# Where the causal mask of two score blocks is written, and in which order the transposed probabilities are copied

## The chip, the cores and the metric

The kernel runs on one core of a Trainium2 chip. A core has engines with instruction queues of their own: TensorE (PE in the profile; its weight loads are listed as PEld), VectorE (DVE), ScalarE (ACT), GpSimd (POOL) and SyncE (SP), which here issues nearly all DMAs. Each engine takes its instructions strictly in the order in which they were written and waits on semaphores of the others. The metric is the device time of one execution in microseconds. The kernel before took 1091.67 us, the median of three runs (1091.38 to 1092.66).

## The reference

Attention with a decay, and behind it a gated feed-forward layer on all 4608 tokens. The sizes: batch 8, 8 heads, 576 positions, head dimension 64; model dimension 512, hidden dimension 2048; all in float32.

```python
def _attn_ref(q, k, v, f):
    scores = scale * np.matmul(q, k.transpose(0, 1, 3, 2))
    log_f = np.log(np.clip(f, 0.0001, 1.0))
    cum = np.cumsum(log_f, axis=-1)
    decay = cum[:, :, :, None] - cum[:, :, None, :]
    causal = np.triu(np.ones((S, S), dtype=bool), k=1)
    scores = np.where(causal, -1000000000.0, scores + decay)
    scores = scores - np.max(scores, axis=-1, keepdims=True)
    attn = np.exp(scores)
    attn = attn / (np.sum(attn, axis=-1, keepdims=True) + 1e-09)
    return np.matmul(attn, v).astype(np.float32)

def _moe_ref(x, w_in, w_out):
    h = x @ w_in
    sp = np.maximum(h, 0.0) + np.log1p(np.exp(-np.abs(h)))
    g = h * erf(sp)
    return (g @ w_out).astype(np.float32)
```

The row's own `cum` cancels in the softmax, so the kernel adds only a term that depends on the key's position. It calls these terms the decays.

## The kernel before

**Two phases.** The first 350 us compute the attention of 64 heads; the rest is the feed-forward layer (class `Moe`), whose lines the change leaves alone. During the attention, the weights of the later phase are also unpacked, combined and written back to memory in small pieces (`convert`), and the first activations are split into high and low parts; that work goes to DVE, ACT and POOL between the attention's own.

**Pairs, halves, steps.** Two heads make a pair p (32 pairs). The 576 rows of a head are cut into five blocks 0 to 4 that end at 64, 192, 320, 448 and 576; because of the causal mask a block i needs only the keys up to its own end. A pair takes two steps t of the loop at L660: the even one has blocks 4 and 1, the odd one blocks 3, 2 and 0. The letter j is the head in the pair.

**A step's pipeline.** In step t the program writes, in this order: `normalize(t - 2)`, `store(t - 5)`, `scores(t)`, the first half of `exps(t - 1)`, the first half of `reduce(t)`, `transposes(t - 3)`, one `evacuate`, `values(t - 4)`, the other halves of `exps` and `reduce`, the other `evacuate`s, and then pieces of the weights' conversion. Since every engine keeps the written order, this order decides who stands behind whom.

- `scores` (L517) is TensorE's: for each block the products of q and k into PSUM (L526), and then for each block and head one constant product (L531): an identity (`eye`) times `upper`, a 128x128 triangle of -2^33 in bfloat16, added onto the block's diagonal. That is the causal mask. There are two PSUM tiles for scores, one per head, so the scores of a step wait for the reductions of the step before.
- `reduce` (L543) is DVE's: it adds the decays `c` to the scores, takes the minimum of the negated row and writes the sum to `pr` in SBUF (L549). Each instruction is followed by a short one that reads the accumulator.
- `exps` (L557) is ACT's, in place in `pr` (L561), with the row's sum.
- `normalize` (L564): DVE adds a small number and takes the reciprocal (L566, L568), POOL multiplies each row block of both heads (L572), in the order of the blocks.
- `transposes` (L575): TensorE turns 128x128 pieces of `pr` into PSUM banks (L584). An even half fills three banks of four pieces, an odd half three banks and a fourth with one piece, that of block 0. There are three bank buffers (`ps_t`).
- `evacuate` (L586) copies a bank to `pt` in SBUF: full banks go to ACT (L593), the third bank of odd halves to DVE (L591), the small fourth bank to DVE (L589, 64 columns).
- `values` (L597) is TensorE's product of `pt` and v (L611), `store` copies it out of PSUM on DVE (L620 to L624) and writes it to memory.

**Decays.** A pair's `c` holds 2 x 576 values, the same in every row, which two DMAs spread over the rows (`load_decays`, L486). They are issued in the even step four steps ahead of the pair's first. Pair 0 has none of them: its decays are made at the start by `spread` (L501) with TensorE and ACT.

**The start.** `lead(n)` (L495) is n products of the identity with itself, whose result nobody reads; each is two instructions in the profile. There are eight at the beginning and four in each of steps 1 and 2.

Of the kernel before, what the change touches and what calls it, by code (L numbers as in the profile page):

```python
# [312 lines left out]
def attention_moe(ctx, tc, q2, k2, vp, f, w_in, w_out, out):  # L313
# [145 lines left out]
    with ExitStack() as ph:  # L459
# [57 lines left out]
        def scores(t):  # L517


            p, half = divmod(t, 2)  # L520
            q, k = pairs[p][:2]
            s = [ps_s.tile([P, 1024], F32, name=f"s{t}_{j}", tag="s") for j in range(2)]
            for at, i, k0, k1 in PARTS[half]:
                for j in range(2):
                    h = slice(64 * j, 64 * j + 64)
                    nc.tensor.matmul(out=s[j][:, at:at + k1 - k0], lhsT=q[h, PAD + START[i]:PAD + END[i]],  # L526
                                     rhs=k[h, k0:k1], start=i > 0, stop=k1 < END[i])
            for j in range(2):
                for i in BLOCKS[half]:
                    first = max(0, START[i])  # L530
                    nc.tensor.matmul(out=s[j][:, SCOL[i] + first:SCOL[i] + END[i]], lhsT=eye,  # L531
                                     rhs=upper[:, first - START[i]:], start=False, stop=i != 3)
            raw_scores[t] = s
            probs[t] = wk.tile([P, TCOLS[half]], F32, name=f"pr{t}", tag=f"pr{half}")
            n = len(BLOCKS[half])
            line = wk.tile([P, 32], F32, name=f"st{t}", tag=f"st{half}")
            stats[t] = line[:, :6 * n].rearrange("p (a j m) -> p a j m", a=3, j=2)

# [36 lines left out]
        def transposes(t, a):  # L575

            half = t % 2
            if a == 0:
                pts[t] = wk.tile([P, 1600 if half else 1536], F32, name=f"pt{t}", tag=f"pt{half}", bufs=1)
# [6 lines left out]
        def evacuate(t, a):  # L586
            b, pt = banks.pop((t, a)), pts[t]
            if a == 3:
                nc.vector.tensor_copy(out=pt[:, 1536:], in_=b[:, 64:128])  # L589
# [4 lines left out]
            if a == len(BANKS[t % 2]) - 1:  # L594
# [56 lines left out]
        lead(8)  # L651
# [8 lines left out]
        for t in range(NH + 2):  # L660
# [11 lines left out]
            if t in (NH - 24, NH - 16):  # L672
                moe.load_wi((t - NH + 24) // 8)
            if there[2]:
                normalize(t - 2)
            if there[5] and t < NH + 2:
# [7 lines left out]
            elif t < 3:  # L684
                lead(4)
# [4 lines left out]
            if there[3]:  # L690
                for a in range(3):
                    transposes(t - 3, a)
                evacuate(t - 3, 0)
            if there[3] and len(BANKS[(t - 3) % 2]) == 4:
                transposes(t - 3, 3)
# [6 lines left out]
            if there[3]:  # L702
                for a in range(1, len(BANKS[(t - 3) % 2])):
# [92 lines left out]
```

## Time and profile before

| what | value |
|---|---|
| time, median of three runs | 1091.67 us (1091.38 to 1092.66) |
| the profiled execution's own time | 1089.61 us |
| its span | 1087.8 us |
| mean granted clock of TensorE | 0.997 |
| loop of the attention, first scores to last | 5.5 to 322 us |
| constant mask products (L531) | 320, in 64 steps |
| granted clock from 12.0 to 18.8 us | 0.50 |
| mean DMA rate over the span | 270 GB/s |

The span is that of one profiled execution. Busy times add up what an engine ran; pipelined matmuls overlap, so starts of rows tell more of TensorE's pace than their lengths. In a row of the timeline, a number in brackets is the idle time in front of it and what ended that.

### The profile page before, as it was taken

How to read it: one execution, taken by the hardware profiler on the slowest of the kernel's cores; microseconds unless marked ns; L12 is line 12 of the kernel's file. 1: busy time of each engine (PE TensorE's matmuls, PEld its weight loads, DVE VectorE, ACT ScalarE, POOL GpSimd, SP SyncE). 2: the span in 40 equal slices, each digit the busy share in tenths (PEclk: the TensorE clock that was granted, in tenths of full speed). 3: DMA queues.
4: the chain of work that ended last, by engine and by line, in shares of the span. 5: the costliest groups of instructions: out<-in, count | busy, mean ns of one | idle time of the engine just before them, and what ended most of it. 6: DMA issues, size and time to landing. Idle time of an engine off the chain costs nothing.

```text
span 1087.8 us, 22066 instructions
## 1 busy us (share of the span) xinstructions
PE 1078.9 (99%) x7592; PEld 952.5 (88%) x7592; DVE 832.0 (76%) x1906; ACT 740.8 (68%) x1593; POOL 703.8 (65%) x824
## 2 busy tenths in 40 slices
PE   8999999999999999999999999999999999999998
PEld 6888888888889889988999888889988998899887
DVE  6788898888765997988897987676776768676665
ACT  4888889888886766567666666666575656656563
POOL 2657678787764969888787878636454554546322
PEclk8999999999999999999999999999999999999999
DMA  8689988899875687887969777785867769584742
GB/s 285 224 260 324 316 294 277 283 352 329 279 227 208 234 304 294 300 331 252 348 240 351 288 265 282 266 307 185 308 248 254 287 229 327 207 321 181 246 190 97
DMA packets 86191, 293.70 MB, mean 270 GB/s; under 512 B 8896, under 2 KB 25280, under 8 KB 73792
## 3 DMA queue, kind: packets, MB, share of 16 engines
q1 hardware_dynamic: 85936, 292.00, 75.7%
q8 instruction: 61, 1.00, 0.3%
q14 instruction: 50, 0.41, 0.1%
q10 hardware_dynamic: 144, 0.29, 0.1%
HBM read 240.73 MB, written 51.53 MB: 269 GB/s over the span
## 4 chain that ended last, share of the span: by engine, by line
PE 94%; DVE 3%; issue 1%; ACT 1%; DMA 1%; SPq 0%; DVEq 0%; ACTq 0%
PE y L234 34%; PE s L526 10%; PE pha L176 9%; PE o L611 9%; PE phx L176 9%; PE phy L176 9%; PE t L584 8%; PE phb L176 4%; PE s L531 2%; DMA xt_d<-xo 1%; DVE u L182 0%; DVE ys L255 0%; DVE pr L549 0%; DVE e L215 0%; DMA k<-in_k_dram 0%
## 5 line engine op out<-in xcount | busy, mean ns | idle before, releaser
L223 POOL TENSOR_TENSOR gl<-e,gh 128x384 fp32r<-128x384 f32 x192 | 217.6, 1165 | 263.3 <-PE y L234 157.4
L234 PE MATMUL y<-wo,gh 128*128 128x512 f32 x1152 | 356.4, 390 | 0.4 <-DVE ys L255 0.3
L234 PEld LDWEIGHTS y<-wo,gh 128*128 128x128 f32 x1152 | 215.0, 188 | 45.5 <-DVE ys L255 1.7
L572 POOL TENSOR_SCALAR pr<-pr,st 128x576 f32<-128x576 f32 (+4 forms) x320 | 164.9, 536 | 104.2 <-DVE st L568 42.7
L234 PE MATMUL y<-wo,gl 128*128 128x512 f32 x576 | 225.1, 391 | 0.0
L255 DVE TENSOR_TENSOR ys<-y,ys 128x512 f32<-128x512 f32 x252 | 172.0, 687 | 55.0 <-PE y L234 53.6
L561 ACT ACTIVATE pr<-pr,st 128x576 f32<-128x576 f32 (+3 forms) x320 | 177.0, 559 | 4.2 <-DVE st L549 4.2
L549 DVE CUSTOM_DVE_ANT_0 pr<-s,c 128x576 f32<-128x576 f32 (+3 forms) x320 | 136.6, 487 | 51.0 <-PE s L531 26.5
L222 ACT CAST gh<-e 128x384 fp32r<-128x384 f32 x192 | 94.0, 513 | 67.2 <-DVE e L215 64.9
L205 ACT ACTIVATE e<-u 128x384 f32<-128x384 f32 x144 | 75.0, 522 | 78.6 <-DVE u L182 75.2
L234 PEld LDWEIGHTS y<-wo,gl 128*128 128x128 f32 x576 | 108.1, 188 | 22.7
L593 ACT COPY pt<-t 128x512 f32<-128x512 f32 x158 | 88.3, 581 | 50.8 <-PE t L584 50.6
L176 PE MATMUL pha<-xs,wi 128*128 128x384 f32 x576 | 116.9, 337 | 0.1
L176 PE MATMUL phx<-xs,wi 128*128 128x384 f32 x576 | 115.4, 334 | 0.0
L176 PE MATMUL phy<-xs,wi 128*128 128x384 f32 x576 | 115.3, 334 | 0.0
L526 PE MATMUL s<-k,q 64*128 64x320 f32 (+4 forms) x768 | 112.6, 412 | 1.6 <-DVE st L549 1.1
L205 ACT ACTIVATE e<-pha 128x384 f32<-128x384 f32 x48 | 23.6, 492 | 125.5 <-PE pha L176 125.5
L176 PEld LDWEIGHTS pha<-xs,wi 128*128 128x128 f32 x576 | 102.3, 188 | 4.2 <-DVE u L186 0.4
L584 PE MATMUL t<-ident,pr 128*128 128x128 f32 x800 | 103.8, 275 | 0.7 <-ACT pt L593 0.6
L611 PE MATMUL o<-pt,v 128*64 128x128 f32 (+1 forms) x1920 | 102.5, 259 | 0.9 <-DVE xo L620 0.9
L611 PEld LDWEIGHTS o<-pt,v 128*64 128x64 f32 x1920 | 93.7, 137 | 10.3 <-DVE st L549 4.4
L526 PEld LDWEIGHTS s<-k,q 64*128 64x128 f32 x768 | 75.1, 189 | 30.3 <-issue 15.2
(73 smaller groups left out, 1758.8 us busy)
## 6 DMA issues: line engine op xcount, KB each, us to landing
wi<-wi_d SPq DMA_DIRECT2D x48, 1792.0 KB, 7.5
wo<-wo_d SPq DMA_DIRECT2D x48, 1024.0 KB, 6.5
v<-in_vp_dram SPq DMA_DIRECT2D x32, 576.0 KB, 4.8
r<-xt_d SPq DMA_DIRECT2D x48, 384.0 KB, 9.1
c<-cum_d SPq DMA_DIRECT2D x62, 288.0 KB, 6.8
q<-in_q_dram SPq DMA_DIRECT2D x32, 320.0 KB, 5.5
k<-in_k_dram SPq DMA_DIRECT2D x32, 288.0 KB, 5.9
part_d<-ys SPq DMA_DIRECT2D x36, 256.0 KB, 6.3
```

What stands on the lines that cost most here:

```text
L176: nc.tensor.matmul(out=ps, lhsT=wi[:, w, n, kd], rhs=xs[:, x, kd], start=not part and kd == 0 and i == 0, stop=kd == 1 and i == 2, skip_gr ...
L205: nc.scalar.activation(out=e_, in_=h[c], func=AF.Softplus)
L222: nc.scalar.copy(out=gh, in_=e_)
L223: nc.gpsimd.tensor_tensor(out=gl, in0=e_, in1=gh.bitcast(F32), op=ALU.subtract)
L234: nc.tensor.matmul(out=y, lhsT=x[:, cs], rhs=wo[:, i, w], start=i == 0 and n == 0, stop=i == 1 and n == 2)
L255: nc.vector.tensor_tensor(out=ys, in0=y, in1=ys, op=ALU.add)
L526: nc.tensor.matmul(out=s[j][:, at:at + k1 - k0], lhsT=q[h, PAD + START[i]:PAD + END[i]], rhs=k[h, k0:k1], start=i > 0, stop=k1 < END[i])
L549: nc.vector.tensor_tensor_reduce(out=to[:, ::-1] if j else to, in0=score, in1=decay_, scale=-0.125, scalar=BIG, op0=ALU.add, op1=ALU.min, ...
L561: nc.scalar.activation(out=seg, in_=seg, func=AF.Exp, bias=st[:, 0, j, m:m + 1], scale=-1.0, accum_out=st[:, 1, j, m:m + 1])
L572: nc.gpsimd.tensor_scalar(out=seg, in0=seg, scalar1=st[:, 2, j, m:m + 1], scalar2=1.0, op0=ALU.mult, op1=ALU.mult)
L584: nc.tensor.transpose(out=b[:, n * P:(n + 1) * P], in_=probs[t][:, at:at + P], identity=ident)
L611: nc.tensor.matmul(out=o[h, to:to + width], lhsT=v[:, ch, h], rhs=pt[:, at[j]:at[j] + width], start=n == 0, stop=n == len(parts) - 1, skip ...
```

## The change

The mask of block 3 in all pairs, and of block 4 in all pairs but the first, no longer goes onto the scores by a product. GpSimd writes the fill value into the decays instead: `mask(p, i)` fills the 128 columns of `c` on the diagonal of block i, for both heads, above the diagonal, with -2^33. It is called in odd steps: block 3 of the same pair ahead of `normalize`, and block 4 of the next pair behind it. The columns of block 3 are also read by block 4's rows (in the even step, without a fill), so their fill comes after those.

In odd halves the small bank with the one piece of block 0 is transposed first and copied first, by ScalarE; the other three banks follow. Only in the last half it stays as it was.

At the start there are eleven constant products instead of eight ahead of the first scores, and four in each of steps 0, 1 and 2.

```diff
@@ scores(t)
                     nc.tensor.matmul(out=s[j][:, at:at + k1 - k0], lhsT=q[h, PAD + START[i]:PAD + END[i]],
-                                     rhs=k[h, k0:k1], start=i > 0, stop=k1 < END[i])
+                                     rhs=k[h, k0:k1], start=i > 0, stop=k1 < END[i] or i == 4 and p > 0)
             for j in range(2):
                 for i in BLOCKS[half]:
+                    if i == 3 or i == 4 and p:
+                        continue
                     first = max(0, START[i])
                     nc.tensor.matmul(out=s[j][:, SCOL[i] + first:SCOL[i] + END[i]], lhsT=eye,
-                                     rhs=upper[:, first - START[i]:], start=False, stop=i != 3)
+                                     rhs=upper[:, first - START[i]:], start=False, stop=True)
...
+        def mask(p, i):
+
+            c = pairs[p][2][:, :, START[i]:END[i]]
+            nc.gpsimd.affine_select(out=c, in_=c, pattern=[[0, 2], [-1, P]], compare_op=ALU.is_ge, fill=MASK,
+                                    base=0, channel_multiplier=1)
@@ transposes(t, a), evacuate(t, a)
-            if a == 0:
+            if t not in pts:
...
             if a == 3:
-                nc.vector.tensor_copy(out=pt[:, 1536:], in_=b[:, 64:128])
+                (nc.vector.tensor_copy if t == NH - 1 else nc.scalar.copy)(out=pt[:, 1536:], in_=b[:, 64:128])
...
-            if a == len(BANKS[t % 2]) - 1:
+            if a == (3 if t == NH - 1 else 2):
                 del probs[t]
@@ before the loop
-        lead(8)
+        lead(11)
@@ the loop
+            if half and there[0]:
+                mask(p, 3)
             if there[2]:
                 normalize(t - 2)
+            if half and t + 1 < NH:
+                mask(p + 1, 4)
...
             if t == 0:
                 spread(pairs[0][2], cum)
-            elif t < 3:
+            if t < 3:
                 lead(4)
...
             if there[3]:
-                for a in range(3):
+                order = range(3) if half else (3, 0, 1, 2)
+                for a in order:
                     transposes(t - 3, a)
-                evacuate(t - 3, 0)
-            if there[3] and len(BANKS[(t - 3) % 2]) == 4:
-                transposes(t - 3, 3)
+                for a in order[:-2]:
+                    evacuate(t - 3, a)
...
             if there[3]:
-                for a in range(1, len(BANKS[(t - 3) % 2])):
+                for a in range(1, 3):
                     evacuate(t - 3, a)
```

Line numbers move in the changed file: L531 is L533 there, L549 is L557, L572 is L580, L584 is L592, and the fill is L544.

On TensorE, an even step (the third pair's) stood like this before: four mask products, the three full banks, then the small one (`t_3`), then the values (`o`).

```order
L531 LDWEIGHTS eye
L531 MATMUL s_0_401<-upper,eye 128x128
L531 LDWEIGHTS eye
L531 MATMUL s_0_401<-upper,eye 128x128
L531 LDWEIGHTS eye
L531 MATMUL s_1_402<-upper,eye 128x128
L531 LDWEIGHTS eye
L531 MATMUL s_1_402<-upper,eye 128x128
L584 MATMUL t_0_421<-ident,pr_255 128x128 x4
L584 MATMUL t_1_426<-ident,pr_255 128x128 x4
L584 MATMUL t_2_431<-ident,pr_255 128x128 x4
L584 MATMUL t_3_437<-ident,pr_255 128x128
```

The same step now:

```order
L533 LDWEIGHTS eye
L533 MATMUL s_0_415<-upper,eye 128x128
L533 LDWEIGHTS eye
L533 MATMUL s_1_416<-upper,eye 128x128
L592 MATMUL t_3_433<-ident,pr_267 128x128
L592 MATMUL t_0_435<-ident,pr_267 128x128 x4
L592 MATMUL t_1_440<-ident,pr_267 128x128 x4
L592 MATMUL t_2_445<-ident,pr_267 128x128 x4
```

Block 4's product of each head is gone (block 1 keeps its own), and the small bank's transpose moved from the end to the front.

On POOL, an odd step had only the six products of `normalize` and then conversion work; `pr` are the probabilities, `st` the row sums, and the names in brackets the engines whose semaphores are waited for.

```order
L572 TENSOR_SCALAR pr_957<-pr_957,st_958 128x448 [waits DVE_49,PE_49,Activation_49]
L572 TENSOR_SCALAR pr_957<-pr_957,st_958 128x448 [waits Activation_49]
L572 TENSOR_SCALAR pr_957<-pr_957,st_958 128x320
L572 TENSOR_SCALAR pr_957<-pr_957,st_958 128x320 [waits Activation_49]
L572 TENSOR_SCALAR pr_957<-pr_957,st_958 128x64
L572 TENSOR_SCALAR pr_957<-pr_957,st_958 128x64 [waits Activation_49]
```

The same step now, with the fill of block 3 in the pair's `c` ahead, and that of block 4 in the next pair's `c` behind:

```order
L544 AFFINE_SELECT c_715<-c_715 128x2x128 [waits DVE_49]
L580 TENSOR_SCALAR pr_979<-pr_979,st_980 128x448 [waits DVE_49,PE_49,Activation_49]
L580 TENSOR_SCALAR pr_979<-pr_979,st_980 128x448 [waits Activation_49]
L580 TENSOR_SCALAR pr_979<-pr_979,st_980 128x320
L580 TENSOR_SCALAR pr_979<-pr_979,st_980 128x320 [waits Activation_49]
L580 TENSOR_SCALAR pr_979<-pr_979,st_980 128x64
L580 TENSOR_SCALAR pr_979<-pr_979,st_980 128x64 [waits Activation_49]
L544 AFFINE_SELECT c_878<-c_878 128x2x128 [waits DMAHW5_49,DMAHW4_49]
```

The first fill waits for DVE, the second for the two DMAs that bring the decays; everything that follows on POOL stands behind both.

At the start, TensorE's order behind the first step's scores was:

```order
L507 MATMUL spread_223<-cum,first 128x512
L507 MATMUL ends<-cum,first 128x64
L507 MATMUL spread_228<-cum,first 128x512
L507 MATMUL ends<-cum,first 128x64
L526 MATMUL s_0_241<-k_168,q_167 128x448
L526 MATMUL s_1_242<-k_168,q_167 128x448
```

Now it is:

```order
L507 MATMUL spread_226<-cum,first 128x512
L507 MATMUL ends<-cum,first 128x64
L507 MATMUL spread_231<-cum,first 128x512
L507 MATMUL ends<-cum,first 128x64
L499 MATMUL lead<-ident 128x128 x4
L526 MATMUL s_0_255<-k_168,q_167 128x448
```

Four constant products stand between the spread and the scores of step 1.

## The prediction

> **What bounds the kernel.** I read the page first: the engines' shares, then the chain that ended last. (In the rows PE is TensorE, PEld its weight loads, DVE VectorE, ACT ScalarE, POOL GpSimd.)
>
> ```profile
> PE 1078.9 (99%) x7592; PEld 952.5 (88%) x7592; DVE 832.0 (76%) x1906; ACT 740.8 (68%) x1593; POOL 703.8 (65%) x824
> ...
> PE 94%; DVE 3%; issue 1%; ACT 1%; DMA 1%; SPq 0%; DVEq 0%; ACTq 0%
> ```
>
> TensorE is busy 99% of the span and is 94% of the chain. Work taken off it shortens the run, as long as nobody makes it wait instead. The change touches only the attention, so I read the chain there in order of time; a row is start, length, line and count.
>
> ```profile
> 31.16 1.66 PE s L526 x12
> ...
> 129.62 1.66 PE s L526 x12
> ...
> 251.58 1.66 PE s L526 x12
> ...
> 286.10 1.50 PE s L526 x12
> ...
> 290.97 1.66 PE s L526 x12
> ...
> 295.95 1.50 PE s L526 x12
> ...
> 320.51 1.66 PE s L526 x12
> ```
>
> The 1.50 rows open even steps, the 1.66 rows odd ones. Undisturbed, an even step lasts 290.97 - 286.10 = 4.87 us and an odd one 4.98 us: 9.85 us a pair. From 31.16 to 320.51 stand 29 pairs, 285.7 us at that pace, and they took 289.35: 3.7 us were lost. All of it lies between 129.62 and 251.58, where 12 pairs took 121.96 us instead of 118.2. Busy time by stretch (columns: length, PE, PEld, DVE, ACT, POOL, clock, DMA share, GB/s):
>
> ```profile
> 31.00:129.00 98.00, 98.00 (x1185) 82.14 (x1183) 79.33 (x317) 83.42 (x254) 62.26 (x111) 1.00 0.85 274
> 129.00:247.00 118.00, 116.64 (x1389) 98.40 (x1387) 102.85 (x375) 102.51 (x303) 97.17 (x155) 1.00 0.89 305
> ```
>
> Ahead of the middle stretch TensorE has no gap at all and POOL is at 64%. In the middle one DVE and ACT are at 87%, POOL at 82%, and they sometimes come late. So TensorE's work is what counts, with less reserve in the middle. What follows the attention, two thirds of the span, holds none of the edited lines, and I leave it as it is.
>
> **The constant products.** A block 3 loses its mask product in all 32 pairs, block 4 in 31, for two heads each: 64 + 62 = 126 products go.
>
> ```profile
> 207.18 0.40 PE L531 MATMUL s<-upper,eye 128*128 128x128 bf16 x4
> 207.41 1.73 PE L584 MATMUL t<-ident,pr 128*128 128x128 f32 x13
> 209.07 0.44 PE L611 MATMUL o<-pt,v 128*64 128x128 f32 x4
> ...
> 212.21 0.46 PE L531 MATMUL s<-upper,eye 128*128 128x128 bf16 x6
> 212.50 1.51 PE L584 MATMUL t<-ident,pr 128*128 128x128 f32 x12
> 213.94 0.44 PE L611 MATMUL o<-pt,v 128*64 128x128 f32 x4
> ```
>
> Lengths overlap in the pipeline, so I use starts. Four products hold TensorE from 207.18 to 207.41, 0.23 us, or 0.0575 each; six, two of them half as wide, take 0.29, the same rate. 126 x 0.0575 = **-7.2 us**. Masks of the other blocks stay, so the change of operand type before them stays too.
>
> **The small bank.** In an even step thirteen transposes take 209.07 - 207.41 = 1.66 us; in an odd one twelve take 1.44, or 0.12 each. The thirteenth thus costs 0.22: 0.10 is a wait. There are three buffers, and the fourth bank waits for the first to be copied out:
>
> ```profile
> 208.11 0.59 ACT L593 COPY pt<-t 128x512 f32<-128x512 f32 x1 [0.45 <-PE t L584]
> L509 ACT COPY c<-ends 128x64 f32<-128x64 f32 x2 | 0.4, 220 | 0.0
> ```
>
> The copy of a full bank runs until 208.70 and only then can the thirteenth go. With the small bank first, its one transpose is done about 0.4 us earlier than four are, its copy takes 0.22 us, inside the 0.45 us for which ACT stood idle, and the bank is needed only after nine transposes, 1.1 us in. So I let the wait go in all 31 such steps: **-3.1 us**; the ends are 0 and, with the longer waits of the middle stretch, 3.8. DVE loses such a copy in 31 steps, ACT gains 31 x 0.22 us. A price stands against it: the small bank needs the last two normalized rows, so its transpose now waits for the end of POOL's six products instead of the first.
>
> **The fill on POOL.** 63 fills come in, two a pair.
>
> ```profile
> L328 POOL TENSOR_SCALAR_AFFINE_SELECT low<-low 128x128 f32<-128x128 f32 x1 | 0.3, 292 | 0.1
> L572 POOL TENSOR_SCALAR pr<-pr,st 128x192 f32<-128x192 f32 x64 | 26.4, 425 | 0.0
> L572 POOL TENSOR_SCALAR pr<-pr,st 128x64 f32<-128x64 f32 x64 | 20.6, 338 | 0.0
> c<-cum_d SPq DMA_DIRECT2D x62, 288.0 KB, 6.8
> ```
>
> The same operation on half the elements takes 0.29 us. 128 more elements cost another POOL operation 0.09 us, which gives 0.38; twice the work gives 0.58. I take 0.4. The decays land 6.8 us after their issue and are issued about three steps, 14 us, before the fill of block 4: no wait there. The fill of block 3 waits for the reductions of the step before, which read those columns; the reductions of its own step wait for it.
>
> ```profile
> 309.28 0.35 DVE L549 CUSTOM_DVE_ANT_0 pr<-s,c 128x192 f32<-128x192 f32 x1
> 310.89 2.84 POOL L572 TENSOR_SCALAR pr<-pr,st 128x448 f32<-128x448 f32 x6 [2.81 <-ACT pt L593]
> 312.71 0.63 DVE L549 CUSTOM_DVE_ANT_0 pr<-s,c 128x448 f32<-128x448 f32 x1 [1.58 <-PE s L531]
> ...
> 202.65 3.29 POOL L572 TENSOR_SCALAR pr<-pr,st 128x448 f32<-128x448 f32 x6
> 205.90 1.16 POOL L412 TENSOR_TENSOR wa<-wa 128x256 f32<-128x256 f32 x1
> ```
>
> In the quiet part the old step's reductions end at 309.63 and the new ones start at 312.71; POOL idles for 2.81 us in between. The fill hides whole, 2.6 us ahead of its reader, and at 313.73 the second fill goes behind the six products and ahead of the weights' subtractions, which nobody on the path awaits. In the middle stretch POOL can have no gap, as from 202.65 on: there the first fill ends near 203.05, the six products at 206.34 instead of 205.94, still 1.1 us before the transposes at 207.41. What is lost there is what queues up. POOL's work grows to 97.2 + 24 x 0.4 = 106.8 us in 118.0 - 12 x 0.33 = 114.0 us (a pair gains 0.23 in products and 0.10 in the wait), 94%; ACT's to 102.5 + 12 x 0.22 = 105.1, 92%. The stretch lost 3.8 us at 82 and 87%; I take 40% more, **+1.5 us**, from ends of 0 and 4.0, its whole gain.
>
> **The start.** Three constant products more ahead of the first scores, four more behind the spread, and the clock:
>
> ```profile
> 1.36 3.78 PE L499 MATMUL lead<-ident 128*128 128x128 f32 x16 [1.36 <-POOL ident masks.py:199]
> 5.54 1.57 PE L526 MATMUL s<-k,q 64*128 64x320 f32 x12 [0.40 <-DMA k<-in_k_dram]
> 9.40 0.33 PE L507 MATMUL ends<-cum,first 64*128 64x64 f32 x2
> 10.44 3.80 PE L526 MATMUL s<-k,q 64*128 64x448 f32 x12 [0.71 <-DVE st L549]
> 16.69 2.81 PE L526 MATMUL s<-k,q 64*128 64x320 f32 x12
> 19.67 1.11 PE L499 MATMUL lead<-ident 128*128 128x128 f32 x8
> 20.95 2.65 PE L526 MATMUL s<-k,q 64*128 64x448 f32 x12 [0.17 <-DVE st L549]
> 5.20:12.00 6.80, 5.66 (x30) 3.36 (x32) 4.00 (x12) 3.10 (x9) 0.00 (x0) 1.00 0.68 241
> 12.00:18.80 6.80, 6.80 (x33) 5.85 (x31) 4.44 (x18) 4.16 (x17) 0.05 (x1) 0.50 0.84 272
> ```
>
> One such product is two instructions: 0.22 us each at the beginning, 0.12 later. Six more from 5.14 end between 5.9 and 6.4, where the scores began at 5.54, and the spread stands right behind those: **+0.4** of 0 to 0.9. The other eight take 1.0 us, from about 9.5; scores waited until 10.44 anyway: **+0.1**. From 12.0 to 18.8 the granted clock is 0.50, after a stretch in which TensorE was busy 5.66 of 6.80 us. The step that ran in it took 16.69 - 10.44 = 6.25 us, the next, mostly past it, 20.95 - 16.69 = 4.26. If the filled gap keeps the clock up, the first costs 2.0 less; the ends are 0 and 3.4, half of the 6.8. I take **-2.0**, since the new work fills 0.7 of the 1.1 us of idle time in front of the half clock. The Trainium skill, TensorE: Matmul & The Clock Gate, section Why this matters for your kernels, asks only that idle gaps between bursts stay under about 3 us. Here no gap between 5.20 and 12.00 is longer than about 0.7 us and the clock fell all the same, so the trace disagrees; by that rule the four products would gain nothing and the sum would be that of the first rival.
>
> **The sum.** -7.2 - 3.1 + 1.5 + 0.4 + 0.1 - 2.0 = -10.3 us. The profiled execution took 1089.61 us (span 1087.8, the rest around it), so 1079.3 on its own time. The three runs shown have a median of 1091.67, 2.06 above it; nothing quoted says why. I set the difference on the median: **1081.4 us**.
>
> **Rivals.** (1) The clock still halves, the rest goes as forecast: -8.3, 1083.4. For it speaks that 0.4 us of the idle time stays, and that no row shows where the clock's threshold lies. Chance 0.27.
>
> (2) The middle stretch gives back more than it gains. DVE can be held by POOL:
>
> ```profile
> 206.40 0.69 DVE L566 TENSOR_TENSOR st<-st,edge 128x4 f32<-128x4 f32 x1
> 212.50 0.16 DVE L566 TENSOR_TENSOR st<-st,edge 128x6 f32<-128x6 f32 x1
> ```
>
> The first ends at 207.09, just when POOL's operation from 205.90 does; alone it takes 0.16. The first fill now stands right behind the reductions, where DVE has such operations. Should half of 24 fills hold DVE for 0.4 us on the path, that is 4.8 us; with POOL at 94% I price the stretch at 5.5 instead of 1.5: -6.3, 1085.4. Against it: DVE idles 13% there and several waits of 0.4 us would fit. Chance 0.17. The Trainium skill, SBUF — State Buffer, section SBUF: two separate sides, has GpSimd and a VectorE operation with two SBUF inputs take one port pair in turns, each for its whole instruction; the trace agrees with the 0.69 us.
>
> (3) The change doesn't do what it says: ACT comes to the small copy so late that the fourth bank waits as before: -7.2, 1084.5. ACT's 0.45 us of idle time speaks against it. Chance 0.08.
>
> (4) Slower: POOL becomes the bound of the middle stretch. It needs 97.2 + 24a us for fills of a us each. Outside the stretch about 8 us are still gained, so the run gets slower once 97.2 + 24a passes 126, at a = 1.2 us. At 1.6 the stretch takes 135.6: 17.6 more, less 8, is 1101. The 0.29 us of the half-sized fill speaks against it. Chance 0.04.
>
> **The numbers.** The forecast has 0.44. The low end takes every good end: -7.2 - 3.8 - 3.4 + 0 + 0.1 is -14.3, 1077.4, and 1 us for what else was lost in the middle: 1076.5. The high end is rival 2 with the clock still halved, 1087.4: 1087.5. Rival 4 and rare sums lie outside. 0.2% is 2.2 us, about what a measurement of this kernel can tell from no change. All cases but the fourth are faster by more; I leave 0.04 for a worse rival 2 that ends within it: 0.92, 0.04, 0.04.
>
> **What would show it.** Undisturbed pairs of 9.52 us (4.66 and 4.86); mask products 194 instead of 320; thirteen transposes in 1.56 us. Fills of about 0.4 us, with no idle time of DVE put down to POOL outside the middle; 12 pairs there in about 119.5 us. A clock of 1.00 from 12.0 to 18.8 and the scores of the third step near 15 instead of 16.69. Wrong would be: pairs still at 9.85 (a wait took the products' place), or reductions that start late behind fills.

## The result, and the profile after

The changed kernel took **1085.44 us**, the median of four runs (1084.94 to 1086.11), against 1091.53 (1089.52 to 1092.66) for the kernel before beside it: a ratio of 0.9939, interval 0.9926 to 0.9952. The forecast was 1081.4 with a range of 1076.5 to 1087.5. The direction and the range held; about 4 us of the expected 10.3 did not come. One run of the kernel before, timed later beside the experiments, took 6054.32 us and is left out of all that follows. The profiled execution has a span of 1083.6 us (1087.8 before). Its page opens with these shares and ends with this chain:

```profile
PE 1072.9 (99%) x7480; PEld 948.4 (88%) x7480; DVE 830.1 (77%) x1875; ACT 746.2 (69%) x1624; POOL 731.5 (68%) x887
...
PE 91%; DVE 5%; POOL 1%; issue 1%; ACT 1%; DMA 1%; SPq 0%; POOLq 0%; DVEq 0%; ACTq 0%
```

TensorE is busy for 6.0 us less, and has less of the chain: DVE's share rose from 3% to 5%, and POOL appears in it. The undisturbed part is as forecast. Two steps of the quiet part from TensorE's timeline (start, length, line, count):

```profile
283.32 1.56 PE L526 MATMUL s<-k,q 64*128 64x320 f32 x12
284.82 0.28 PE L533 MATMUL s<-upper,eye 128*128 128x128 bf16 x2
284.94 1.59 PE L592 MATMUL t<-ident,pr 128*128 128x128 f32 x13
286.46 1.54 PE L619 MATMUL o<-pt,v 128*64 128x128 f32 x28
287.94 1.73 PE L526 MATMUL s<-k,q 64*128 64x448 f32 x12
...
292.80 1.56 PE L526 MATMUL s<-k,q 64*128 64x320 f32 x12
```

The masks and the fills from the view by source line (count, and least, median and longest duration in ns):

```profile
L533 PE MATMUL s<-upper,eye x194: 192/219/230, 8.1 to 318.2; 128*128 128x128 bf16 x130, 128*128 128x64 bf16 x64
...
L544 POOL TENSOR_SCALAR_AFFINE_SELECT c<-c x63: 397/407/864, 12.2 to 315.4; 128x256 f32<-128x256 f32 x63
```

The pair takes 292.80 - 283.32 = 9.48 us (forecast 9.52), the even step 4.62, the odd one 4.86; thirteen transposes take 286.46 - 284.94 = 1.52 us (1.56); 194 mask products are left; a fill takes 0.41 us. So the pace is right, and the kernel doesn't hold it. Busy time by stretch, from the scores of the sixth step to those of the last (length, PE, PEld, DVE, ACT, POOL, clock, DMA share, GB/s), first of the kernel before:

```profile
31.09:129.55 98.46, 98.46 (x1195) 82.60 (x1192) 79.79 (x319) 83.88 (x256) 62.72 (x113) 1.00 0.86 275
129.55:251.51 121.96, 120.60 (x1431) 101.72 (x1428) 106.78 (x384) 106.02 (x314) 100.69 (x158) 1.00 0.89 304
251.51:320.44 68.93, 68.93 (x837) 57.82 (x833) 51.90 (x214) 59.38 (x180) 47.20 (x83) 1.00 0.80 274
```

and of the changed one:

```profile
30.08:126.56 96.48, 96.06 (x1155) 81.14 (x1151) 79.44 (x304) 85.66 (x267) 70.24 (x131) 1.00 0.86 279
126.56:248.83 122.27, 119.98 (x1384) 101.11 (x1381) 107.01 (x377) 107.95 (x326) 112.05 (x182) 1.00 0.88 304
248.83:316.38 67.55, 66.98 (x810) 56.72 (x806) 50.48 (x204) 60.53 (x187) 53.57 (x100) 1.00 0.84 281
```

The stretches hold ten, twelve and seven pairs. At the undisturbed pace (9.84 us before, 9.48 after) they would take 98.4, 118.1, 68.9 before and 94.8, 113.8, 66.4 after. Before, 0.1 + 3.9 + 0.0 = 4.0 us were lost against that; now 1.7 + 8.5 + 1.2 = 11.4. The middle stretch is not a bit shorter, although TensorE has 48 products less in it. DVE stands out there: its twelve small copies went to ACT, and it is as busy as before. One group of it tells a part of why, in the middle stretch of before and then of after (busy us, mean ns):

```profile
L566 DVE TENSOR_TENSOR st<-st,edge 128x6 f32<-128x6 f32 (+1 forms) x24 | 5.9, 246 | 0.7 <-ACT pr L561 0.6
```

```profile
L574 DVE TENSOR_TENSOR st<-st,edge 128x6 f32<-128x6 f32 (+1 forms) x25 | 10.2, 407 | 0.6 <-ACT pr L569 0.6
```

The addition on six numbers a row, which takes 0.16 us when alone, went from 0.25 to 0.41 us on average. Nothing in it was edited; POOL beside it was.

These 4.3 us in one group are not 4.3 us more in DVE's sum, for other DVE operations of the stretch were held less (L376 took 5.7 us there before and 3.3 after). The fairer comparison is among kernels whose small copies stand on ACT too (all below). Three without fills in the middle stretch (small bank alone, no fills, no fills in the middle) have DVE busy for 105.6 to 105.7 us there and take 120.6 to 120.9. Three with fills (the whole change, only block 3, eight products at the start) have it busy for 107.0 to 109.0 and take 122.3 to 123.5. The stretch grows by about as much as DVE's busy time.

### The profile page after: what moved, and what is told of

Its sections match the earlier page's. It is cut to its first block, busy times and chain, and to the rows that moved or that the text cites. A ratio compares the mean times of both kernels' runs of the same rounds, so it can differ in the third digit from the quotient of the medians.

```text
span 1083.6 us, 21937 instructions
## 1 busy us (share of the span) xinstructions
PE 1072.9 (99%) x7480; PEld 948.4 (88%) x7480; DVE 830.1 (77%) x1875; ACT 746.2 (69%) x1624; POOL 731.5 (68%) x887
## 4 chain that ended last, share of the span: by engine, by line
PE 91%; DVE 5%; POOL 1%; issue 1%; ACT 1%; DMA 1%; SPq 0%; POOLq 0%; DVEq 0%; ACTq 0%
PE y L234 35%; PE pha L176 9%; PE phx L176 9%; PE phy L176 9%; PE s L526 8%; PE o L619 8%; PE t L592 6%; PE phb L176 5%; DVE pr L557 1%; PE s L533 1%; POOL pr L580 1%; DVE wtop L384 1%; DMA c<-cum_d 1%; PE lead L499 1%; DVE wtop L377 0%
## 5 line engine op out<-in xcount | busy, mean ns | idle before, releaser
L580 POOL TENSOR_SCALAR pr<-pr,st 128x576 f32<-128x576 f32 (+4 forms) x320 | 167.3, 543 | 55.0 <-ACT pt L601 21.5
L557 DVE CUSTOM_DVE_ANT_0 pr<-s,c 128x576 f32<-128x576 f32 (+3 forms) x320 | 136.6, 487 | 47.6 <-PE s L533 19.4
L526 PE MATMUL s<-k,q 64*128 64x320 f32 (+4 forms) x768 | 115.8, 408 | 1.5 <-DVE st L557 1.1
L526 PEld LDWEIGHTS s<-k,q 64*128 64x128 f32 x768 | 77.8, 187 | 30.6 <-issue 14.6
L176 PEld LDWEIGHTS phx<-xs,wi 128*128 128x128 f32 x576 | 101.2, 188 | 0.3 <-DVE u L182 0.3
```

The costliest lines, as they stand in the source:

```text
L176: nc.tensor.matmul(out=ps, lhsT=wi[:, w, n, kd], rhs=xs[:, x, kd], start=not part and kd == 0 and i == 0, stop=kd == 1 and i == 2, skip_gr ...
L557: nc.vector.tensor_tensor_reduce(out=to[:, ::-1] if j else to, in0=score, in1=decay_, scale=-0.125, scalar=BIG, op0=ALU.add, op1=ALU.min, ...
L580: nc.gpsimd.tensor_scalar(out=seg, in0=seg, scalar1=st[:, 2, j, m:m + 1], scalar2=1.0, op0=ALU.mult, op1=ALU.mult)
```

## The experiments

All times are medians. The kernel before was timed beside each group of experiments and had medians of 1089.4 to 1089.9, with runs from 1086.8 up, since its start varies (below); the whole change was timed only beside the 1091.53. So I compare the kernels with one another by median, and by the three stretches of their profiles (5 to 25, 25 to 49, 49 to 63, counted in steps):

| kernel | median, us | ratio to before, interval | stretches, us |
|---|---|---|---|
| before | 1091.53 | | 98.46, 121.96, 68.93 |
| the whole change | 1085.44 | 0.9939 [0.9926, 0.9952] | 96.48, 122.27, 67.55 |
| start alone | 1088.34 | 0.9977 [0.9967, 0.9987] | 98.42, 122.15, 68.90 |
| small bank alone | 1086.16 | 0.9964 [0.9950, 0.9979] | 97.17, 120.58, 68.85 |
| fills alone | 1090.78 | 1.0007 [0.9992, 1.0022] | 97.58, 124.74, 68.12 |
| change without the addition | 1082.21 | 0.9921 [0.9908, 0.9934] | 95.52, 121.13, 66.91 |
| change without fills | 1084.07 | 0.9951 [0.9933, 0.9969] | 97.18, 120.55, 68.23 |
| every fill twice | 1093.00 | 1.0030 [1.0017, 1.0044] | 97.35, 128.30, 68.61 |
| no fills in the middle | 1083.26 | 0.9941 [0.9919, 0.9963] | 96.36, 120.94, 67.50 |
| change without POOL's subtractions | 1078.35 | 0.9899 [0.9879, 0.9920] | 95.15, 118.97, 66.61 |
| no fills, no addition | 1082.38 | 0.9937 [0.9920, 0.9953] | 97.07, 119.82, 68.18 |
| only block 3 filled | 1085.97 | 0.9966 [0.9955, 0.9977] | 96.24, 123.35, 68.09 |
| eight products at the start | 1085.01 | 0.9963 [0.9946, 0.9980] | 96.56, 123.49, 67.62 |
| last version | 1079.75 | 0.9905 [0.9890, 0.9921] | 95.52, 119.07, 66.86 |

A stretch is from one execution. The loop of the kernel with eight products at the start is that of the whole change: its middle stretch took 1.2 us more, the other two agree within 0.1. The loop of start alone is that of before, and all three agree within 0.2. So I read differences of the middle stretch only above about 1.2 us.

### The three parts, one at a time

**The start alone**: before, with

```diff
-        lead(8)
+        lead(11)
-            elif t < 3:
+            if t < 3:
                 lead(4)
```

> The kernel before with the seven constant products alone. Theory clock: the half clock from 12.0 to 18.8 us goes, as in the changed kernel's trace, where it never comes; the first scores start 0.8 us later, and the fifth step's scores near 30.3 us instead of 31.1; time 0.7 to 1 us under a kernel before whose trace looks like the one shown, and up to 3 us under the median of the runs before, if those have a longer half clock. Rival, the start gains nothing of its own and comes from fewer products: 1091 or more, half clock back.

Measured 1088.34 (eight runs within 1.7 us), 1.5 below the kernel before in that group. The loop took what it took before, the sixth step's scores stand 1.5 us earlier (29.55 instead of 31.09), and the clock stayed full from 5.6 us on.

**The small bank alone**: before, with the edits of `transposes`, `evacuate` and their order.

> The kernel before with the small bank first and on ScalarE, alone. If the wait of the fourth bank goes everywhere: 3 us less than before (thirteen transposes take 1.56 us instead of 1.66), since POOL and VectorE have no more to do than before. If VectorE's bursts of conversion work set the pace between 130 and 252 us (theory burst), the 12 pairs there still take 122 us and the gain is only that of the other pairs, 1.5 to 2 us.

Measured 1086.16, with runs from 1083.64 to 1090.06: 3.7 below the kernel before in that group, where 3 was expected. The profiled execution had the slowest start of all: its second step's scores stood at 13.76 us and its third's at 21.21, 7.45 us later, where the whole change needs 4.11. So its stretches tell more: 1.3 and 1.4 us less in the first two and 0.1 in the third (0.7 there without fills but with the new start, further below).

**The fills alone**: before, with the masks' edits in `scores`, `mask` and its two calls.

> The kernel before with the fills on GpSimd instead of 126 products, alone. All products gained would be 7.2 us. Theory port (fills push POOL's other work so that it stands beside VectorE's two-input additions and holds them) and theory full (POOL is too busy and the fills themselves come late): the 12 pairs between 130 and 252 us gain nothing or lose, the rest gains 0.23 us a pair, so 2.5 to 4 us less than before. The additions of the row sums (two inputs in SBUF) take 0.4 us in the mean there, 0.25 before.

Measured 1090.78, no change that can be told (0.9992 to 1.0022); the 2.5 to 4 us expected did not come. The fills win 0.9 and 0.8 us in the quiet stretches, where their 0.23 us a pair would be 2.3 and 1.6, and lose 2.8 in the middle.

### The addition left out

```diff
-            nc.vector.tensor_tensor(out=st[:, 1], in0=st[:, 1], in1=tiny[:, :2 * n].rearrange("p (j m) -> p j m", j=2),
-                                    op=ALU.add)
```

> The changed kernel without VectorE's addition of 1e-9 to the row sums (a sum is at least 1, so float32 drops it); the reciprocal stays. Theory port: VectorE no longer has a two-input operation in every step that POOL can hold; in the 12 pairs between 130 and 252 us that frees 10 us of VectorE's time and 4 us or more of TensorE's: 1080 to 1082. Theory full: POOL is as busy as before the edit, its fills still come late, gain under 1.5 us: 1084 to 1085.5. Theory burst: VectorE's work falls from 87% to 79% of those pairs, also 1081, but then the kernel before gains as much from the same edit, which a later run tells.

Measured 1082.21, 3.2 below the whole change. In the first and the last stretch more than half of the lost time is back (95.52 and 66.91 us, where the undisturbed pace gives 94.8 and 66.4); in the middle it is 1.1 us, no more than one profile differs from another. So this held operation is a part of the loss and not the whole. The waits of DVE in its middle stretch show what took its place (us, times, longest):

```profile
DVE pr L557 <- POOL c L544: 7.1, 6, 2.8
```

The reductions now come sooner and wait for the fills instead; in the whole change that row has 2.3 us, three times.

### Without fills, with twice the fills, and with fills in the quiet part only

The kernel without fills is before with the two other parts. In the one with twice the fills, `mask` issues each twice:

```diff
-            nc.gpsimd.affine_select(out=c, in_=c, ...
+            for _ in range(2):
+                nc.gpsimd.affine_select(out=c, in_=c, ...
```

and in the third, pairs 12 to 24 keep their products:

```diff
-            if half and there[0]:
+            if half and there[0] and not 12 <= p < 25:
                 mask(p, 3)
-            if half and t + 1 < NH:
+            if half and t + 1 < NH and not 12 <= p + 1 < 25:
                 mask(p + 1, 4)
```

> The change without its fills: the constant mask products stay on TensorE, the small bank comes first and the start is filled. Theory 'fills give back' (the fills win their 0.23 us a pair where POOL has room and lose more than that in the twelve pairs of the middle stretch, by POOL's operations beside DVE's two-input ones and by POOL's own lateness): the middle stretch takes 119.5 to 121, less than the 122.3 with fills, the other stretches 97.2 and 68.8 instead of 96.5 and 67.6, so 1085 to 1086.5, level with the whole change. The forecast's sum (fills worth 7.2 less 1.5): 5.7 more than the whole change, 1091. Theory 'bursts' (DVE's conversions set the pace of the middle whatever else): middle stretch 122.3 as with fills, others up by 0.23 a pair, 1089.

> Every fill is issued twice in a row, 63 more POOL operations of 0.41 us that change nothing in the data. Theory 'fills give back': in the middle stretch POOL's work goes from 112 to 122 us in 122; the stretch gets at least 5 us longer, the others under 1 us each; 1091 to 1096, and DVE waits for fills more often. Theory 'bursts': POOL's work is not what counts, 1085 to 1086.5. Forecast's rival of POOL as the bound (time decided by the sum of POOL's work): about 1.0 us per 0.4 us beyond a full stretch, at least 1090.

> The whole change, but pairs 12 to 24 (the middle stretch) keep their mask products and get no fills. Theory 'fills give back': middle stretch 120.6 as in the kernel with the small bank alone, the other stretches 96.5 and 67.6 as with the change, 1083.5 to 1084.5, faster than the whole change by 1 to 2. The forecast (a fill is worth 0.23 a pair less little): 1.5 to 3 slower than the whole change, 1087 to 1088.5. Theory 'bursts': level, 1085 to 1086.

Without fills the time is 1084.07, 1.4 us below the whole change: the fills, which should have brought 7.2 less 1.5, bring nothing here. With fills only in the quiet part it is 1083.26, a little below the 1083.5 to 1084.5 of the theory that they give back. With twice the fills it is 1093.00, and the reason is another one. The middle stretch:

```profile
127.05:255.35 128.30, 122.09 (x1385) 101.14 (x1381) 107.49 (x377) 107.96 (x325) 123.96 (x206) 1.00 0.86 289
```

and DVE's first wait in it:

```profile
DVE pr L558 <- POOL c L545: 17.8, 13, 3.0
```

POOL is busy for 124.0 of 128.3 us, 97%, and the reductions wait 17.8 us for fills: here POOL is the bound. In the whole change it is at 112.1 of 122.3, 92%, and the same wait is 2.3 us. So the fourth rival's mechanism exists, but the loss of the change is not yet that one.

### POOL's subtractions left out

```diff
-        nc.gpsimd.tensor_tensor(out=top, in0=top, in1=hi.bitcast(F32), op=ALU.subtract)
...
-            nc.gpsimd.tensor_tensor(out=w, in0=w, in1=highs[a][:, lo % 4:lo % 4 + hi - lo].bitcast(F32), op=ALU.subtract)
```

> The whole change without the weights' low parts: POOL's two subtractions in place (L404 and L422, 13.3 us of its 112 in the middle stretch) are left out, so the low parts keep the full values. Theory 'fills give back': POOL is back at about 81% there, DVE's L384 and L375 fall from 1.14 and 0.80 us to 0.9 and 0.55, and the middle stretch falls to 117 to 119, the time to 1080 to 1082. Theory 'bursts': DVE's conversions are all still there, the stretch stays within 1 us of 122.3 and the time at 1084.5 to 1086.

Measured 1078.35, with the fills and DVE's own work all there:

```profile
30.31:125.46 95.15, 95.15 (x1155) 80.63 (x1151) 77.24 (x306) 85.43 (x266) 61.48 (x123) 1.00 0.87 283
125.46:244.43 118.97, 117.67 (x1383) 98.72 (x1381) 99.93 (x375) 108.03 (x326) 99.88 (x173) 1.00 0.91 312
244.43:311.04 66.61, 66.61 (x809) 56.62 (x805) 49.54 (x204) 60.46 (x187) 46.49 (x92) 1.00 0.85 283
```

DVE's busy time in the middle falls from 107.0 to 99.9 us for nearly the same operations (377 and 375); the quiet stretches run within 0.4 us of the undisturbed pace. There POOL was busy only 70.24 of 96.48 us in the whole change, so it was not short of time: what counted is beside whom its long operations stand.

How much of this is the fills' doing? The kernel without fills loses only 0.2 and 0.3 us in the two quiet stretches against its own undisturbed pace of 9.70 us a pair. So the 2.3 us that come back there (96.48 to 95.15 and 67.55 to 66.61) could hardly be had without fills: it is the fills and the subtractions together that cost them. In the middle 3.3 us come back and 5.2 stay lost, and the kernel without fills loses 4.1 there too; the subtractions were not left out of that kernel, so the fills' share of the 3.3 is not shown.

One place shows the way it goes, the eleventh step. First POOL and DVE of the whole change (start, length):

```profile
52.45 0.41 POOL L544 TENSOR_SCALAR_AFFINE_SELECT c<-c 128x256 f32<-128x256 f32 x1
52.83 1.28 POOL L404 TENSOR_TENSOR wtop<-wtop,wohi 128x512 f32<-128x512 f32 x1
...
53.41 1.25 DVE L384 SCALAR_TENSOR_TENSOR wtop<-wraw,wtop 128x512 int32<-128x512 int32 x1
...
57.29 0.75 DVE L557 CUSTOM_DVE_ANT_0 pr<-s,c 128x576 f32<-128x576 f32 x1
```

Then the same place without fills:

```profile
52.81 1.28 POOL L404 TENSOR_TENSOR wtop<-wtop,wohi 128x512 f32<-128x512 f32 x1
...
53.83 0.81 DVE L384 SCALAR_TENSOR_TENSOR wtop<-wraw,wtop 128x512 int32<-128x512 int32 x1
...
57.28 0.75 DVE L549 CUSTOM_DVE_ANT_0 pr<-s,c 128x576 f32<-128x576 f32 x1
```

and without the subtractions:

```profile
53.64 0.69 DVE L384 SCALAR_TENSOR_TENSOR wtop<-wraw,wtop 128x512 int32<-128x512 int32 x1
...
56.95 0.75 DVE L555 CUSTOM_DVE_ANT_0 pr<-s,c 128x576 f32<-128x576 f32 x1
```

With the fills DVE reaches L384 at 53.41, 0.42 us earlier than without them: that is the time that the products have given. But the fill has put POOL's L404 behind itself, so that it ends at 54.11, and DVE's operation ends 0.55 us behind that, at 54.66 (without fills 0.55 behind 54.09, at 54.64). The next reductions start at 57.29 and 57.28: the lead is gone. Without the subtraction the operation takes 0.69 us, its length beside an idle POOL.

TensorE meets this delay twice in the step. First the whole change, then without fills:

```profile
54.00 1.57 PE L526 MATMUL s<-k,q 64*128 64x320 f32 x12
...
57.42 1.54 PE L619 MATMUL o<-pt,v 128*64 128x128 f32 x28 [0.21 <-DVE xo L632]
58.90 2.15 PE L526 MATMUL s<-k,q 64*128 64x448 f32 x12
...
64.19 1.57 PE L526 MATMUL s<-k,q 64*128 64x320 f32 x12
```

```profile
54.49 1.56 PE L526 MATMUL s<-k,q 64*128 64x320 f32 x12
...
57.74 1.54 PE L611 MATMUL o<-pt,v 128*64 128x128 f32 x28
59.21 1.83 PE L526 MATMUL s<-k,q 64*128 64x448 f32 x12
...
64.29 1.57 PE L526 MATMUL s<-k,q 64*128 64x320 f32 x12
```

Its values (`o`) wait for a copy of `store` that stands behind the conversions and the addition in DVE's order, and its next scores, 2.15 us instead of 1.83, wait for the reductions. Of the 0.49 us by which it led at 54.00, 0.10 are left at 64.19. By the starts of TensorE's rows, 1.6 of the 2.9 us lost in the quiet stretches stand in front of values, the rest in scores.

### Is it the addition that the fills lengthen?

Before with start and small bank, and without the addition.

> The kernel without fills, and without DVE's addition of 1e-9 to the sums (which are at least 1). With the fills this addition was worth 3.2 us. Theory 'port' (the fills keep POOL busy while DVE adds, so DVE is held): without fills the additions are held less, 7.3 us in all in the middle stretch against 10.2, and leaving them out gains 1.5 to 2.5: 1081.6 to 1082.6. Theory 'the add costs the same with or without fills' (it is held by the weights' subtractions alone): 3.2 gained, 1080.5 to 1081.2. Theory 'bursts' (such short operations set nothing): under 0.8 gained, 1083.3 to 1084.3.

Measured 1082.38: 1.7 us gained, where it was 3.2 with fills. So, by these medians of different groups, nearly half of what the addition costs in the whole change is owed to the fills. By the stretches it costs 0.1, 0.7 and 0.05 us without fills and 1.0, 1.1 and 0.6 with them: in the quiet part nearly all of it is. One step in which the addition is held, the 46th, DVE and then POOL of the whole change:

```profile
229.04 1.38 DVE L377 TENSOR_SCALAR wtop<-wtop 128x512 int32<-128x512 int32 x1
230.34 1.23 DVE L574 TENSOR_TENSOR st<-st,edge 128x6 f32<-128x6 f32 x1
...
228.70 2.85 POOL L422 TENSOR_TENSOR wa<-wa,whi 128x512 f32<-128x512 f32 x2
```

and without fills:

```profile
226.64 2.92 DVE L375 TENSOR_SCALAR wtop<-wraw 128x512 int32<-128x512 int32 x1
...
230.40 0.16 DVE L566 TENSOR_TENSOR st<-st,edge 128x6 f32<-128x6 f32 x1
...
226.77 2.50 POOL L422 TENSOR_TENSOR wa<-wa,whi 128x512 f32<-128x512 f32 x2
```

With fills, POOL's two subtractions end at 231.55 and the addition at 231.57; without, they are over at 229.27 and the addition takes 0.16 us. But without fills L375 is held before that, 2.92 us instead of 0.42; with them it takes 0.48 and L377 is held, 1.38 instead of 0.43. The time held in this step is about the same, 2.2 and 2.5 us, and TensorE's values come late in both. So this step shows that the addition is held by what stands beside it, and not what the fills cost.

### Which fill, and how much of the start

In the first kernel `mask(p + 1, 4)` is left out and block 4 keeps its product; in the second `lead(11)` is `lead(8)`.

> The whole change, but only block 3 is filled; block 4 keeps its product in every pair. Theory 'order' (the fill of block 4, written behind the normalization and ahead of the weights' subtractions, is what pushes POOL's long operations beside DVE's): the middle stretch falls to 119.2 to 119.8, the others are 96.6 and 67.7, 1082 to 1083. Theory 'sum of POOL's work' (it does not matter which fill, each costs its time where POOL has no room): the middle stretch about 121.4, halfway between 120.6 without fills and 122.3 with both, the others halfway too, 1084 to 1085.2. The other way round (the fill of block 3, ahead of the normalization and right behind the reductions, costs most): the middle stretch 122 or more, 1085.5 or more.

> The whole change with eight constant products ahead of the first scores, as before, and the four behind the spread as changed. Theory 'the gap' (the half clock came from the idle time around the spread, which the four products fill): the clock stays full, first scores at 5.5 instead of 6.3, sixth step's scores up to 0.8 earlier than 30.1, 1084.6 to 1085.4. Theory 'the phase' (when the clock comes up depends on the work before the scores as a whole): in some runs the clock halves again, the runs spread over 4 us or more, median 1085.5 to 1088.

With block 3 alone filled: 1085.97, nothing regained, and the middle stretch is no shorter than with both. I had thought the fill of block 4 the worse one, since it stands right ahead of the subtractions; that fell. With eight products at the start: five of nine runs took 1084.13 to 1085.01, three about 1086.7, and one 1090.33 with a mean clock of 0.995. The four products behind the spread seem to do most, but only with the three in front as well did every kernel keep its runs within 2 us.

### A version from all this

No addition, and in pairs 12 to 24 the product for block 3 again:

```diff
-                    if i == 3 or i == 4 and p:
+                    if i == 3 and not 12 <= p < 25 or i == 4 and p:
                         continue
...
-            if half and there[0]:
+            if half and there[0] and not 12 <= p < 25:
                 mask(p, 3)
```

> The change without DVE's addition of 1e-9, and with block 3 of pairs 12 to 24 (the middle stretch) masked by its product again, so that only block 4 is filled there; outside both are filled. The other stretches should take 95.5 and 66.9 as with both fills and no addition, the tail 766.5, and the sixth step's scores come at 30: the time is 960.7 plus the middle stretch, which was 121.1 with both fills and 119.8 with none. If block 3's fill alone does the harm and block 4's is hidden: 118.4 to 119, 1079 to 1079.8. If block 4's fill gains and loses the same: 119.8, 1080.5. If each fill costs half of the difference: 120.5 to 121, 1081.2 to 1081.8.

Measured **1079.75** (1079.37 to 1080.03), 0.9905 of the kernel before and 5.7 us below the change. Its middle stretch:

```profile
124.81:243.88 119.07, 117.68 (x1408) 99.68 (x1405) 97.85 (x351) 107.78 (x326) 107.70 (x170) 1.00 0.91 312
```

119.07 us, against 121.13 with both fills and 119.82 with none: in the middle block 3's fill did the harm, 2.1 us here and 2.5 by the medians, as the first of the three expectations had it, and block 4's does none that shows.

## Why the prediction came out as it did

- **The constant products, -7.2: right in size.** 194 are left, and the undisturbed pair is 0.22 us shorter by them (9.70 without fills, 9.48 with). This is a gain of pace, and it was given back: 29 pairs at 0.22 are 6.4 us, and the 29 pairs of the loop took 285.96 without fills and 286.30 with them.
- **The small bank, -3.1: right, a little low.** The even step without fills takes 4.73 instead of 4.87, 0.14 for the 0.10 forecast, and thirteen transposes no longer wait. From the start alone to the kernel without fills the 29 pairs go from 289.47 to 285.96, 3.5 us, and the medians by 4.3. The longest of these waits, in one step of the middle stretch, did not go: the thirteen transposes take 2.34 us there before and 2.20 in the changed kernel. So the gain beyond 3.1 is the 0.14 a step, and not the longer waits on which the upper end of 3.8 was put. The third rival, that ACT comes too late, is out.
- **The give-back, +1.5: this is the term that failed.** Lost time in the 29 pairs went from 4.0 to 11.4 us (4.7 without fills): 7.4 in place of 1.5, past the end of 4.0. Two steps of the argument were wrong. First, POOL's lack of room was taken as the only cost, by shares of busy time, and only for the middle stretch; but 2.8 of the 7.4 us were lost in the quiet stretches, at 73% and 79%. Second, the prediction let POOL's subtractions be put off, since "nobody on the path awaits" them. Nobody awaits their results, but DVE's conversions and the addition take longer while they run (0.69 to 1.25 us, 0.16 to 1.23 in the steps shown). A later subtraction runs beside a later DVE operation, and behind that one, in DVE's order, stand the copies and the reductions that TensorE waits for. In the quiet stretches the runs show this. In the middle they show that block 3's fill costs 2 us or more; how it does so there is in part argued. One sign that the prediction named appeared as well, but once: reductions waited for a fill in the third stretch, for 1.6 us.
- **The second rival was that mechanism,** and its time, 1085.4, is the one measured. It was given a chance of 0.17 on the ground that DVE idles 13% in the middle. That idle time is no cover: it stands in front of reductions that wait for scores, behind the held operations and not beside them. The rival too had the wrong place: it saw the first fill itself hold DVE for 0.4 us, and in the middle alone; in the step shown it is POOL's subtraction of 1.28 us, pushed by the fill, that holds it. That the rival's figure and the measured one agree to 0.1 us is luck: the 2.8 us lost outside the middle, the microsecond more from the small bank and the median of before cancel in it.
- **The start, -1.5 net: right in kind, about 0.7 too much in the profile.** Start alone gained 1.5 by the medians. This is TensorE of the changed kernel:

```profile
1.36 5.06 PE L499 MATMUL lead<-ident 128*128 128x128 f32 x22 [1.36 <-POOL ident masks.py:199]
6.34 1.82 PE L526 MATMUL s<-k,q 64*128 64x320 f32 x12
...
10.72 1.16 PE L499 MATMUL lead<-ident 128*128 128x128 f32 x8
11.81 2.47 PE L526 MATMUL s<-k,q 64*128 64x448 f32 x12
...
15.92 0.77 PE L526 MATMUL s<-k,q 64*128 64x320 f32 x2 [0.39 <-PE lead L499]
```

  and these are two stretches of it, the second with the times that were at half clock before:

```profile
6.90:12.00 5.10, 5.10 (x33) 3.36 (x30) 1.65 (x5) 2.04 (x6) 0.00 (x0) 1.00 0.56 224
12.00:18.80 6.80, 6.04 (x39) 4.30 (x39) 5.74 (x23) 5.26 (x21) 0.81 (x2) 1.00 0.89 263
```

  The clock no longer halves, and the second step takes 15.92 - 11.81 = 4.11 us instead of 6.25: 2.1, for the 2.0 forecast. So the first rival is out. But the first scores come 0.80 later (+0.4 forecast), the spread's last products stand at 10.47 instead of 9.40, and the eight instructions start behind them at 10.72, where about 9.5 was forecast. So the second step's scores are 1.37 later in all where 0.5 was forecast, and the third step's 0.77 earlier where 1.5 was. The sixth step's scores stand 1.0 us earlier than before.
- **The fourth rival's price was too kind.** It let the run get slower than before from 1.2 us a fill. At twice 0.41 it is slower already (1093.00).
- **Against which number.** The sum was set on the median of before, 2 us above its profiled execution with nothing to explain that. That choice flatters the forecast: between the two profiled executions the gain is 4.2 us (3.05 in the 29 pairs, 1.0 ahead of them), and against the later medians of before, 1089.4 to 1089.9, it is 4.0 to 4.5, where 10.3 was forecast. The runs of the kernel before lay between 1086.8 and 1094.3 in the groups, and the start is the likely reason: those with a mean clock of 0.995 have a median of 1092.1, those with 1.000 one of 1087.8. The mean clock does not tell all of them apart, for five runs with 1.000 took 1092.2 to 1094.3; in the profile of small bank alone, whose mean is also 1.000, the half clock lasted until 21.1 us and is not counted in that mean.

Not settled: how the middle stretch's loss divides between DVE held beside POOL and fills that come late themselves (leaving out the addition turned one into the other), what the subtractions cost there without fills, and why block 3's fill harms more than block 4's. It stands ahead of the normalization and behind the reductions of the step before, which may make all of POOL's later work wait, but no run tried it at another place.

## What to carry to other kernels

An operation moved to an engine that has idle time on average can cost more than its own length when it pushes that engine's other work: look at which operations of a third engine slow down beside that work, and where these stand on the path, before calling the move hidden. Compare the pace of undisturbed steps with the length of whole stretches, before and after; when the pace improves as worked out and the stretch does not, the time has gone into the disturbed steps. And decide it stretch by stretch: here the same fills paid a little in the quiet pairs (1083.26 against 1084.07 without any) and cost in the middle.

## What the runs showed of the hardware

- DVE beside POOL: a conversion with one input (L375, 128x512) took 2.92 us beside two of POOL's subtractions, and 0.42 in the quiet part; one with two inputs (L384) took 0.69, 0.81 or 1.25, and ended 0.55 us behind POOL's operation in both of the last two; an addition of 128x6 took 0.16 alone and 1.23 beside a subtraction, until 0.02 us behind its end. DVE's waits don't show this: it appears only as longer operations. The Trainium skill, SBUF — State Buffer, section SBUF: two separate sides, says that GpSimd and a VectorE instruction, one with two SBUF inputs or one in a two-port mode, take a shared pair of ports for a whole instruction each. The trace agrees, for the conversions with one input too; the time that is left behind POOL's end, 0.55 of 0.69 us for L384 and 0.02 of 0.16 for the addition, is less than the operation's length alone.
- The granted clock at the start differs from one execution to the next of the same kernel, and a few constant products more, ahead of the first steps and within them, kept it full: the runs of such a kernel then lay within 0.7 to 1.9 us of each other, where those of the kernel before varied by 7. The profiles show the full clock from 5.2 us (before), 6.9 (the change), 9.5 (fills alone) and 21.1 (small bank alone); in before it halved again from 12.0 to 18.9, and in fills alone from 12.9 to 23.1. A busy TensorE did not bring it up at once: in small bank alone it was busy for 15.02 of the 15.06 us from 6.04 to 21.10, and eight instructions of constant products took 2.00 us at 19.27, where eight take 1.16 in the changed kernel. The Trainium skill, TensorE: Matmul & The Clock Gate, Part 1, says that the window by which the clock is set runs freely, not from the kernel's start, so that the same kernel warms up at different times; these starts agree with it, though each is of another kernel (before and small bank alone differ only from the fourth step on).
